# Norm applies ahead of the w1 scale, low halves of w1 and w2 on GpSimd, loads ahead of the transposing transfers, and a last tile in two banks

## The chip, the cores and the metric

The kernel runs on one core of a Trainium2 chip. A core has a matrix engine (TensorE, PE in the profile; its weight loads are listed as PEld), a vector engine (VectorE, DVE), an activation engine (ScalarE, ACT), a general engine (GpSimd, POOL) and a sequencer that here issues the transfers (SyncE, SP). The engines run their own queues in order and meet through semaphores. The metric is the device time of one execution in microseconds, the median of the timed runs.

## The reference

The input x has S = 2048 rows of D = 448 numbers. The output is the sum of x, a spectral branch and a mixer branch, both fed by a layer norm over the row.

```python
def _A_ref(x, w_r, w_i):                       # spectral branch
    X = jnp.fft.rfft2(x, axes=(-2, -1))
    return jnp.fft.irfft2(X * (w_r + 1j * w_i), s=(S, D), axes=(-2, -1))

def _B_ref(x, w1, w2, w3, w4):                 # mixer branch
    h = _gelu(_layernorm(x) @ w1)
    # four column groups of h, shifted by +1, -1, +2 and -2 rows, zeros at the ends
    hs = jnp.concatenate([g0, g1, g2, g3], axis=-1) @ w2
    x1 = x + hs
    return x1 + _gelu(_layernorm(x1) @ w3) @ w4

return x + _A_ref(_layernorm(x), A_w_r, A_w_i) + _B_ref(_layernorm(x), B_w1, ...)
```

w1 and w2 are 448 x 448, w3 is 448 x 1792, w4 is 1792 x 448. All inputs are float32.

## The kernel before

**Tiles.** Row 16·a + b of x lies in partition a of tile b, so there are 16 tiles of 128 rows, and a shift by one row is a step to the neighbouring tile. The tiles are worked in four groups, `GRP = [[14, 15, 0, 1], [2, 3, 4, 5], [6, 7, 8, 9], [10, 11, 12, 13]]`. Two tiles share one load (`xt`, 448 KB).

**Number format.** Products run in float16 with each operand split into a high half (the value rounded to float16) and a low half (what is left). A product is three matmuls: high by high, high by low, low by high. A weight is first multiplied by a power of two, which comes from its sum of squares: `squares` (L233 to L237) sums on ACT, `powers` (L239 to L252) reduces on DVE, sums over the partitions with a matmul by ones and makes the powers of two by integer steps on DVE. `split_w` (L257 to L260) then writes the high half on ACT (L258) and the low half on DVE (L259), for w1, w2, w3 and w4 alike.

**Stages.** At the start, PE runs 28 warm-up matmuls on zeros (L732) while the first loads land, and two more behind the product of w1's scale. For each group, `norm1` (L291) takes the row statistics on DVE, makes a rough inverse root with a few tiny DVE steps that end in `nma` (L305), and applies them to the four tiles of the group (L310 on ACT, L312 on DVE or POOL, as its list of engines says). A refinement of the inverse root, tiny steps on POOL (L321 to L341), corrects the scale later. `transpose_split` (L356) turns the four tiles by PE transposes into banks of the accumulation memory (L362), writes the high half on ACT (L365) and the low half on DVE (L366). `w1_in` (L395) makes the products with w1 (matmuls L398), `w1_unit` (L408) applies gelu (L416), splits the result into `hs` (L417, L418) and sends it through a transposing transfer into `hT` (L421). `w2_tile` (L425) makes the product with w2 for one row tile, with four shifted sources (L437), and adds it to x (L439). `ln2` (L442) is the second norm, whose split rows go through transposing transfers too (L473). `front` and `back` (L674, L688) are the w3 and w4 products of a group of two row tiles G, in seven steps of two column blocks f; the w4 products of a row tile accumulate in one bank over all 14 blocks (L696), which is read at the last step (L703), and the result is stored (L705). The spectral branch runs in between: a fold and a first transform (L491 to L528), 16 chunks (L575 to L629) and the inverse (L641 to L669). PE has the w3 and w4 products of the groups as filling for these stages.

**What sets the order.** The program is written in a Python order, and a scheduler of the framework orders the instructions of each engine by priorities, dependences and its own planned time. `behind(key)` makes what is issued inside it come after a named instruction in that plan; `prio` sets a priority. Banks come from tags with two buffers each (tr, mm, acc, sp). SP issues all loads, stores and transposing transfers, one after another in its own order. Eight semaphores count their completions, and each transfer waits for the one eight before it.

**The order around the start.** SP loads group 0 of x, w1 (`w1s`, four parts, the last in two halves), group 1, w2, group 2 and the first two row blocks of w3 (`w3raw`). Group 3 of x and the third row block of w3 are issued behind the last transposing transfer of group 0 (L783 to L785), the last row block of w3 and half of w4 behind those of group 1 (L801 to L804). The scale of w1 (L757) is written behind the norm of group 0 (L756). Group 0's w1 products use three of the four row blocks of w1 first (L768); the last follows between transposes of group 1 (L776 to L780). The low halves of w2 are made when the statistics of group 2 are through (L794 to L796).

Of the kernel before, what the change touches and what calls it, by code (L numbers as in the profile page):

```python
# [20 lines left out]
NB, NC = 16, 16  # L21
# [4 lines left out]
SHIFT = [1, -1, 2, -2]  # L26
WARM = 28, 2
ZPRE = 2.0 ** -7
# [91 lines left out]
def body(tc, nc, x, wf, w1, w2, w3, w4, c_g, c_n, c_small, out):  # L120
# [41 lines left out]
    def xb(b):  # L162
        return xt[b // 2][:, b % 2]
# [69 lines left out]
    def squares(col, src, junk=None):  # L233

        n = src.shape[-1]
        junk = x2mem if junk is None else junk
        A.activation(out=junk[:src.shape[0], :n], in_=src, func=AF.Square, scale=2.0 ** -20, accum_out=col)  # L237

    def powers(m, n, key, tag="acc"):  # L239

        t = pc.tile([128, 2], F32, name=f"pt{key}")
        V.tensor_reduce(out=t[:, 0:1], in_=m[:, :n], axis=AX.X, op=ALU.add)
        pm = bank(tag, f"pm{key}")
        i = T.matmul(pm[:, 0:1], ones, t[:, 0:1], start=True, stop=True)
# [46 lines left out]
    def norm1(g, apply):  # L291
# [15 lines left out]
        for k, b in enumerate(bs):  # L307
            y_, m_ = y[:, n + k:n + k + 1], nm[:, k:k + 1]
            if apply[k] is A:
                A.activation(out=xb(b), in_=xb(b), func=AF.Identity, scale=y_, bias=m_)  # L310
            else:
                i = apply[k].tensor_scalar(out=xb(b), in0=xb(b), scalar1=y_, scalar2=m_, op0=ALU.mult, op1=ALU.add)  # L312
                if apply[k] is V:
                    after["n", g] = (i.ins,)
# [41 lines left out]
    def transpose_split(srcs, dst, key, ts=range(4), at=0, tags=("tr",) * 4):  # L356
        c = slice(128 * at, 128 * at + 128 * len(srcs))
        for t in ts:
            pt = bank(tags[t], f"pt{key}{t}")
            w = 128 if t < 3 else 64  # L360
            for i, s in enumerate(srcs):
                T.transpose(pt[:w, 128 * i:128 * i + 128], s[:, 128 * t:128 * t + w], ident)  # L362
            pt = pt[:w, :128 * len(srcs)]
# [30 lines left out]

    def w1_in(g, i, pm, ts):  # L395
        for t in ts:
            for wi, xi in ((0, 0), (0, 4), (4, 0)) if t < 3 else ((0, 0), (4, 0)):
                T.matmul(pm[:, :D], xTs[g][:, xi + t, 128 * i:128 * i + 128], w1p[:, wi + t],  # L398
                         start=t == 0 and wi + xi == 0, stop=t == 3 and wi == 4)

# [3 lines left out]

    hs_buf.append(x2mem[:, F:F + 1024].rearrange("p (i k n) -> p i k n", i=2, k=4))
    P.memset(hs_buf[HS].rearrange("p i k n -> p (i k) n")[:, :, 112:], 0.0)

    def w1_unit(g, i, pm=None):  # L408
        if pm is None:
            pm = bank(("mm", "mm", "acc", "acc")[i], f"pw1_{g}{i}")  # L410
            w1_in(g, i, pm, range(4))
        c = CS[GRP[g][i]]
        pm = pm[:, :D]
        pv_ = pm.rearrange("p (k n) -> p k n", k=4)
        h = hs_buf[c % (HS if g == 3 else HS + 1)]
        A.activation(out=pm, in_=pm, func=AF.Gelu_apprx_tanh, scale=gsc[:, c:c + 1])  # L416
# [271 lines left out]
    def back(G, fp):  # L688
        h = hs.pop((G, fp))
        if fp == 0:  # L690
            acc[G] = [bank("acc", f"acc{G}{i}") for i in range(2)]
        for i in range(2):
            for f in (2 * fp, 2 * fp + 1):
                for n, (hi, wi) in enumerate(((0, 0), (0, 1), (1, 0))):
                    o = 256 * (f % 2) + 128 * i
                    m = T.matmul(acc[G][i][:, :D], h[:, hi, o:o + 128], w4p[0][:, wi, f],  # L696
                                 start=f == 0 and n == 0, stop=f == 13 and n == 2)
                    after["m", G, fp] = (m.ins,)
            b = 2 * G + i
            if fp == 6 and b in rest:  # L700
                t = rest.pop(b)
                with prio(EVAC):
                    V.scalar_tensor_tensor(out=t, in0=acc[G][i][:, :D], scalar=p34[:, 1:2], in1=t,  # L703
                                           op0=ALU.mult, op1=ALU.add)
                    SY.dma_start(ov[:, b], t)  # L705
            elif fp == 6:
# [26 lines left out]

    warm_up(WARM[0])
    m1, m2, m3, m4 = (pc.tile([128, n], F32, name=f"m{i}") for i, n in ((1, 4), (2, 1), (3, 4), (4, 7)))
    junk4 = row().bitcast(F16)[:, :2 * D]
    V.memset(m2, 0.0)
# [15 lines left out]

    for t in range(4):
        squares(m1[:, t:t + 1], w1s[:, t])
    n1 = [norm1(0, [P, V, A, V])]  # L756
# [188 lines left out]
```

## Time and profile before

| | |
|---|---|
| timed runs | 424.54, 425.66, 427.21 us; median 425.66 |
| profiled execution | 428.35 us, of which the span from the first to the last instruction is 426.6 |
| TensorE clock granted, mean | 0.996 |
| PE matmuls | busy 412.9 us, 97% of the span, 3289 instructions |
| DVE | busy 291.7 us, 68% |
| ACT | busy 248.6 us, 58% |
| POOL | busy 107.8 us, 25% |
| transfers | 47.6 MB, mean 112 GB/s |

The profile is one execution. A line such as `L312 POOL TENSOR_SCALAR xt<-xt,vy,nma x8: 704/715/2584` reads: line 312 of the kernel, on GpSimd, a tensor by scalar operation from xt, vy and nma into xt, eight times, shortest, median and longest in ns. In the timeline a row begins with its start and its length in us; a group of equal instructions in a row is one row with their number behind an x. In square brackets stands how long the engine had been idle before, and which instruction ended the wait. SPq, POOLq and the like are the sequencers' own rows. The row of a transfer is the time that SP spent on issuing it; when its bytes had landed is told apart from it.

### The profile page before, as it was taken

How to read it: one execution, taken by the hardware profiler on the slowest of the kernel's cores; microseconds unless marked ns; L12 is line 12 of the kernel's file. 1: busy time of each engine (PE TensorE's matmuls, PEld its weight loads, DVE VectorE, ACT ScalarE, POOL GpSimd, SP SyncE). 2: the span in 40 equal slices, each digit the busy share in tenths (PEclk: the TensorE clock that was granted, in tenths of full speed). 3: DMA queues.
4: the chain of work that ended last, by engine and by line, in shares of the span. 5: the costliest groups of instructions: out<-in, count | busy, mean ns of one | idle time of the engine just before them, and what ended most of it. 6: DMA issues, size and time to landing. Idle time of an engine off the chain costs nothing.

```text
span 426.6 us, 8457 instructions
## 1 busy us (share of the span) xinstructions
PE 412.9 (97%) x3289; PEld 288.1 (68%) x3289; DVE 291.7 (68%) x619; ACT 248.6 (58%) x428; POOL 107.8 (25%) x191
## 2 busy tenths in 40 slices
PE   7989899999999999999999999999999999999996
PEld 3545465666657777777778878787776767577764
DVE  3889399989854567663478889876899619852122
ACT  4588479974486767553288888864444424522331
POOL 2446520101122964420021211220454303200000
PEclk9999899999999999999999999999999999999999
DMA  8939995454682247223145665520001103430001
GB/s 278 314 75 210 189 274 155 80 126 86 88 198 64 88 137 255 90 83 104 33 112 158 154 166 153 137 70 15 2 2 48 40 2 111 149 129 28 18 0 45
DMA packets 51688, 47.61 MB, mean 112 GB/s; under 512 B 33920, under 2 KB 46912, under 8 KB 51648
## 3 DMA queue, kind: packets, MB, share of 16 engines
q1 hardware_dynamic: 51648, 47.07, 41.6%
q8 instruction: 26, 0.43, 0.4%
q14 instruction: 14, 0.11, 0.1%
HBM read 35.52 MB, written 3.67 MB: 92 GB/s over the span
## 4 chain that ended last, share of the span: by engine, by line
PE 54%; DVE 8%; issue 3%; DMA 3%; ACT 1%; POOL 1%; DVEq 0%; SPq 0%
PE pw L372 22%; PE acc L696 22%; PE ps L523 3%; PE pu L625 2%; PE pp L580 2%; PE px L597 2%; DMA xr<-x 2%; DVE xt L669 1%; DMA out<-xr 1%; DVE xr L480 1%; DVE vh L661 1%; DVE e L657 1%; DVE x2mem L480 1%; DVE e L655 1%; DVE U L638 1%
## 5 line engine op out<-in xcount | busy, mean ns | idle before, releaser
L372 PE MATMUL pw<-x2mem,w3p 128*128 128x256 f16 x1232 | 152.6, 273 | 0.0
L696 PE MATMUL acc<-w4p,hf 128*128 128x448 f16 x672 | 140.1, 353 | 1.0 <-DVE hf L684 1.0
L372 PEld LDWEIGHTS <-w3p 128*128 128x128 f16 x1232 | 118.9, 98 | 24.6 <-issue 0.9
L696 PEld LDWEIGHTS <-hf 128*128 128x128 f16 x672 | 65.2, 98 | 51.9 <-DVE hf L684 1.9
L684 DVE SCALAR_TENSOR_TENSOR hf<-pw,h,hf 128x512 f16<-128x512 f32 x56 | 41.9, 747 | 60.8 <-ACT hf L683 60.5
L681 ACT ACTIVATE pw<-pw,pe 128x512 f32<-128x512 f32 x56 | 36.6, 654 | 68.2 <-PE pw L372 67.2
L437 PE MATMUL pw<-w2p,h 112*128 112x448 f16 x192 | 41.0, 357 | 2.3 <-DMA h<-hs 2.2
L683 ACT ACTIVATE hf<-pw,h 128x512 f16<-128x512 f32 x56 | 38.4, 686 | 1.5
L398 PE MATMUL pw<-w1p,xT 128*128 128x448 f16 x176 | 36.4, 360 | 1.4 <-ACT xT L365 0.8
L606 POOL TENSOR_TENSOR z<-te 128x450 f32<-128x450 f32 x16 | 16.3, 1017 | 73.9 <-DVE te L604 73.9
L437 PEld LDWEIGHTS <-h 112*128 112x128 f16 x192 | 18.9, 99 | 18.2 <-DMA h<-hs 3.2
L398 PEld LDWEIGHTS <-xT 128*128 128x128 f16 x176 | 17.3, 100 | 18.4 <-issue 2.0
L653 POOL TENSOR_TENSOR e<-e 128x226 f32<-128x226 f32 x16 | 13.5, 842 | 56.5 <-ACT e L650 45.3
L587 ACT ACTIVATE pf<-pp 64x450 f16<-64x450 f32 x32 | 17.3, 540 | 16.6 <-DVE pf L588 8.1
L588 DVE TENSOR_TENSOR pf<-pp,pf 64x450 f16<-64x450 f32 x32 | 19.9, 621 | 5.3 <-ACT pf L587 5.0
L650 ACT ACTIVATE e<-pe 128x452 f32<-128x452 f32 x16 | 8.7, 547 | 15.6 <-DVE vh L661 12.3
L602 ACT ACTIVATE te<-px 64x450 f32<-64x450 f32 x32 | 17.2, 538 | 0.5
L660 ACT ACTIVATE vh<-e 128x448 f16<-128x448 f32 x16 | 9.2, 574 | 14.2 <-DVE e L658 10.7
L503 POOL TENSOR_TENSOR xr<-xf 128x452 f32<-128x452 f32 x8 | 9.2, 1155 | 30.9 <-issue 23.4
L514 DVE TENSOR_TENSOR xh<-f,xh 128x452 f16<-128x452 f32 x16 | 11.8, 780 | 6.8 <-ACT xh L513 6.8
L506 POOL TENSOR_TENSOR f<-xr 128x452 f32<-128x452 f32 x16 | 15.9, 1017 | 0.6
L416 ACT ACTIVATE pw<-pw,gsc 128x448 f32<-128x448 f32 x16 | 9.3, 606 | 10.7 <-POOL xt L312 5.7
(155 smaller groups left out, 600.3 us busy)
## 6 DMA issues: line engine op xcount, KB each, us to landing
wc<-wf SPq DMA_DIRECT2D x32, 225.0 KB, 3.5
wl<-wf SPq DMA_DIRECT2D x8, 450.0 KB, 3.8
xt<-x SPq DMA_DIRECT2D x8, 448.0 KB, 5.2
xf<-x SPq DMA_DIRECT2D x8, 448.0 KB, 3.8
w3raw<-w SPq DMA_DIRECT2D x3, 896.0 KB, 11.3
xr<-x SPq DMA_DIRECT2D x12, 224.0 KB, 2.6
out<-xr SPq DMA_DIRECT2D x12, 224.0 KB, 1.9
gn<-c_g SPq DMA_DIRECT2D x16, 128.0 KB, 3.3
```

The costliest lines, as they stand in the source:

```text
L372: T.matmul(ps_out, wp[:, wi + t, cols], xT[:, xi + t, tok], start=t == 0 and wi + xi == 0, stop=t == 3 and wi == 4)
L398: T.matmul(pm[:, :D], xTs[g][:, xi + t, 128 * i:128 * i + 128], w1p[:, wi + t], start=t == 0 and wi + xi == 0, stop=t == 3 and wi == 4)
L437: T.matmul(pm[:, :D], hT[g][:112, 4 * hi + k, o:o + 128], w2p[:, wi, k], start=n == 0, stop=n == 11)
L506: P.tensor_tensor(out=f[:, :, k:k + 2].rearrange("p b s d -> p s b d"), in0=u[:, :, 0], in1=u[:, :, 1], op=op)
L587: A.activation(out=hi, in_=src, func=AF.Copy)
L588: V.tensor_tensor(out=lo, in0=src, in1=hi, op=ALU.subtract)
L602: A.activation(out=e[64 * h:64 * h + 64], in_=px_[64 - 64 * h:128 - 64 * h, :2 * DF], func=AF.Copy)
L606: P.tensor_tensor(out=z, in0=t[:, 0], in1=t[:, 1], op=ALU.add)
L681: A.activation(out=pm, in_=pm, func=AF.Gelu_apprx_tanh, scale=r3)
L683: i = A.activation(out=h[:, 0], in_=pm, func=AF.Copy, scale=h3)
L684: j = V.scalar_tensor_tensor(out=h[:, 1], in0=pm, scalar=h3, in1=h[:, 0], op0=ALU.mult, op1=ALU.subtract)
L696: m = T.matmul(acc[G][i][:, :D], h[:, hi, o:o + 128], w4p[0][:, wi, f], start=f == 0 and n == 0, stop=f == 13 and n == 2)
```

## The change

Five things are changed.

The order of loads: group 3 of x and the third row block of w3 go out right behind the first two row blocks of w3, and the second half of w1's last row block goes out behind group 1 of x.

The start: w1's scale (`powers`) is placed behind the norm of group 0, the two warm-up matmuls behind the scale are left out, the squares write their unused result to another buffer (`xr`), the four transposes of one bank are chained behind those of the bank before, group 0's w1 products run over all four row blocks in passes (high by high, low x, low w) over the four units, and group 1's transposes follow them as three blocks and one. The gelus of group 0 are placed behind group 1's split.

The low halves: w1's row blocks 2 and 3 and all four of w2 are split with a new path, in which GpSimd multiplies the weight in place by its scale, ACT copies it to the high half, and GpSimd subtracts.

Buffers and banks: two `hs` buffers lie in `x2mem` instead of one, the units of group 1 and the transposes of group 2 use other bank tags, w2's scale uses 64 free columns of a bank of group 0, and `w2_tile` takes the shifts in the order 2, 0, 1, 3.

The end: the last row tile (b = 15) accumulates its two halves of 224 columns in two banks, and reads and stores each half by itself.

```diff
-WARM = 28, 2
+WARM = 28
...
-    for h in range(2):
-        SY.dma_start(w1s[64 * h:64 * h + 64, 3], w1[384:448])
+    SY.dma_start(w1s[0:64, 3], w1[384:448])
     load_x(1)
+    SY.dma_start(w1s[64:128, 3], w1[384:448])
...
     load_w3([0, 1])
+    load_x(3)
+    load_w3([2])
...
-        junk = x2mem if junk is None else junk
+        junk = xr.bitcast(F16) if junk is None else junk
...
-        pm = bank(tag, f"pm{key}")
+        pm = bank(tag, f"pm{key}") if isinstance(tag, str) else tag
...
-    def split_w(hi, lo, src, s):
+    def split_w(hi, lo, src, s, low=None):
+        if low is P:
+            P.tensor_scalar(out=src, in0=src, scalar1=s, scalar2=0.0, op0=ALU.mult, op1=ALU.add)
+            i = A.activation(out=hi, in_=src, func=AF.Copy)
+            j = P.tensor_tensor(out=lo, in0=src, in1=hi, op=ALU.subtract)
+            return i.ins, j.ins
...
-            for i, s in enumerate(srcs):
-                T.transpose(pt[:w, 128 * i:128 * i + 128], s[:, 128 * t:128 * t + w], ident)
+            with behind("T", key) if ("T", key) in after else contextlib.nullcontext():
+                for i, s in enumerate(srcs):
+                    m = T.transpose(pt[:w, 128 * i:128 * i + 128], s[:, 128 * t:128 * t + w], ident)
+            after["T", key] = (m.ins,)
...
+    def w1_in(g, units, ts, passes=range(3)):
+        for p in passes:
+            for t in ts:
+                for i, pm in units:
+                    wi, xi = ((0, 0), (0, 4), (4, 0))[p]
+                    if t < 3 or p != 1:
+                        T.matmul(pm[:, :D], xTs[g][:, xi + t, 128 * i:128 * i + 128], w1p[:, wi + t],
+                                 start=t == 0 and p == 0, stop=t == 3 and p == 2)
...
-    hs_buf.append(x2mem[:, F:F + 1024].rearrange("p (i k n) -> p i k n", i=2, k=4))
-    P.memset(hs_buf[HS].rearrange("p i k n -> p (i k) n")[:, :, 112:], 0.0)
+    for o in (0, 1024):
+        hs_buf.append(x2mem[:, o:o + 1024].rearrange("p (i k n) -> p i k n", i=2, k=4))
+        P.memset(hs_buf[-1].rearrange("p i k n -> p (i k) n")[:, :, 112:], 0.0)
...
-            pm = bank(("mm", "mm", "acc", "acc")[i], f"pw1_{g}{i}")
+            pm = bank(("tr" if g == 1 else "mm", "acc")[i // 2], f"pw1_{g}{i}")
...
-        for k in range(4):
+        for k in (2, 0, 1, 3):
...
+            if G == 7:
+                acc[G].append(bank("sp", "acc72"))
...
+            c = D // 2 if b == NB - 1 else D
+            parts = [(slice(o, o + c), acc[G][i + o // c][:, 0:c]) for o in range(0, D, c)]
+            for r, to in parts:
+                with behind("m", G, fp) if (G, fp) == (7, 6) and ("m", G, fp) in after else contextlib.nullcontext():
+                    for f in (2 * fp, 2 * fp + 1):
+                        for n, (hi, wi) in enumerate(((0, 0), (0, 1), (1, 0))):
+                            o = 256 * (f % 2) + 128 * i
+                            m = T.matmul(to, h[:, hi, o:o + 128], w4p[0][:, wi, f, r],
+                                         start=f == 0 and n == 0, stop=f == 13 and n == 2)
...
+                    for r, to in parts:
+                        V.scalar_tensor_tensor(out=t[:, r], in0=to, scalar=p34[:, 1:2], in1=t[:, r],
+                                               op0=ALU.mult, op1=ALU.add)
+                        SY.dma_start(ov[:, b, r], t[:, r])
...
-                        tags=("tr", "tr", "acc", "acc"))
+                        tags=("mm", "mm", "tr", "tr") if g == 2 else ("tr", "tr", "acc", "acc"))
...
     n1 = [norm1(0, [P, V, A, V])]
-    s1, r1 = powers(m1, 4, "1")
-    with behind("p1"):
-        warm_up(WARM[1])
+    with behind("n", 0):
+        s1, r1 = powers(m1, 4, "1", "mm")
...
-    T1(0)
     for t in range(4):
+        with behind("p1"):
+            T1(0, [t])
         with behind("a0", t):
-            after["w1", t] = split_w(w1p[:, t], w1p[:, 4 + t], w1s[:, t], s1)
+            after["w1", t] = split_w(w1p[:, t], w1p[:, 4 + t], w1s[:, t], s1, P if t > 1 else V)
...
-    for t in range(3):
-        for k in range(4):
-            w1_in(0, k, first[k], [t])
+    for t in range(4):
+        w1_in(0, list(enumerate(first)), [t])
     n1[0][0]()
+    with behind("w1", 1):
+        n1.append(norm1(1, [P, V, A, V]))
     with behind("w1", 3):
-        n1.append(norm1(1, [P, V, A, V]))
         squares(m2[:112], flat(w2s[:112]))
-        s2, r2 = powers(m2, 1, "2")
+    T1(1, range(3))
+    with behind("n", 1):
+        s2, r2 = powers(m2, 1, "2", first[0][:, 448:512])
     with behind("p2"):
-        T1(1, range(2))
-        for k in range(4):
-            w1_in(0, k, first[k], [3])
-        T1(1, range(2, 4))
-    for k in range(4):
-        w1_unit(0, k, first[k])
-    with behind("h", 0, 3):
-        load_x(3)
-        load_w3([2])
-    n1[1][0]()
+        T1(1, [3])
...
+    n1[1][0]()
     with behind("a1"):
+        w1_unit(0, 0, first[0])
         n1.append(norm1(2, [P, V, A, P]))
-    with behind("a1"), behind("c", 2):
+    with behind("a1"), behind("n", 2):
+        for k in range(1, 4):
+            w1_unit(0, k, first[k])
+    with behind("na", 2):
         for k in range(4):
-            split_w(w2p[:, 0, k], w2p[:, 1, k], w2s[:112, k], s2[:112])
+            split_w(w2p[:, 0, k], w2p[:, 1, k], w2s[:112, k], s2[:112], P)
```

More of the change, by code (lines that the diff above doesn't have):

```diff
@@ L309, in norm1 @@
             if apply[k] is A:
-                A.activation(out=xb(b), in_=xb(b), func=AF.Identity, scale=y_, bias=m_)
+                i = A.activation(out=xb(b), in_=xb(b), func=AF.Identity, scale=y_, bias=m_)
+                after["na", g] = (i.ins,)
             else:
@@ L393, in h_at @@
         return 128 * i if g else 144 * i + 16
[L395 to L399, printed above, removed]
+    def w1_in(g, units, ts, passes=range(3)):
[6 more added lines that the diff above has]
+                                 start=t == 0 and p == 0, stop=t == 3 and p == 2)
     hs_buf = [p1.tile([128, 2, 4, 128], F16, name=f"hs{i}") for i in range(HS)]
@@ L403, in body @@
         P.memset(t.rearrange("p i k n -> p (i k) n")[:, :, 112:], 0.0)
-    hs_buf.append(x2mem[:, F:F + 1024].rearrange("p (i k n) -> p i k n", i=2, k=4))
-    P.memset(hs_buf[HS].rearrange("p i k n -> p (i k) n")[:, :, 112:], 0.0)
+    for o in (0, 1024):
+        hs_buf.append(x2mem[:, o:o + 1024].rearrange("p (i k n) -> p i k n", i=2, k=4))
+        P.memset(hs_buf[-1].rearrange("p i k n -> p (i k) n")[:, :, 112:], 0.0)
     def w1_unit(g, i, pm=None):
         if pm is None:
-            pm = bank(("mm", "mm", "acc", "acc")[i], f"pw1_{g}{i}")
-            w1_in(g, i, pm, range(4))
+            pm = bank(("tr" if g == 1 else "mm", "acc")[i // 2], f"pw1_{g}{i}")
+            w1_in(g, [(i, pm)], range(4))
         c = CS[GRP[g][i]]
@@ L414, in w1_unit @@
         pv_ = pm.rearrange("p (k n) -> p k n", k=4)
-        h = hs_buf[c % (HS if g == 3 else HS + 1)]
+        h = hs_buf[c % (HS if g == 3 else HS + 2)]
         A.activation(out=pm, in_=pm, func=AF.Gelu_apprx_tanh, scale=gsc[:, c:c + 1])
@@ L691, in back @@
             acc[G] = [bank("acc", f"acc{G}{i}") for i in range(2)]
+            if G == 7:
+                acc[G].append(bank("sp", "acc72"))
         for i in range(2):
[L693 to L698, printed above, removed]
-            b = 2 * G + i
+            b = 2 * G + i
+            c = D // 2 if b == NB - 1 else D
[7 more added lines that the diff above has]
+                                         start=f == 0 and n == 0, stop=f == 13 and n == 2)
+                after["m", G, fp] = (m.ins,)
             if fp == 6 and b in rest:
@@ L702, in back @@
                 with prio(EVAC):
-                    V.scalar_tensor_tensor(out=t, in0=acc[G][i][:, :D], scalar=p34[:, 1:2], in1=t,
-                                           op0=ALU.mult, op1=ALU.add)
-                    SY.dma_start(ov[:, b], t)
+                    for r, to in parts:
+                        V.scalar_tensor_tensor(out=t[:, r], in0=to, scalar=p34[:, 1:2], in1=t[:, r],
+                                               op0=ALU.mult, op1=ALU.add)
+                        SY.dma_start(ov[:, b, r], t[:, r])
             elif fp == 6:
@@ L732, in warm_up @@
             T.matmul(wps, wsrc[:, 0:128], wsrc, start=True, stop=True)
-    warm_up(WARM[0])
+    warm_up(WARM)
     m1, m2, m3, m4 = (pc.tile([128, n], F32, name=f"m{i}") for i, n in ((1, 4), (2, 1), (3, 4), (4, 7)))
     junk4 = row().bitcast(F16)[:, :2 * D]
+    V.memset(m1, 0.0)
     V.memset(m2, 0.0)
@@ L752, in w4_split @@
         split_w(w4p[0][:, 0, f:f + 2], w4p[0][:, 1, f:f + 2], w4raw[:, f:f + 2], s4)
-    for t in range(4):
+    for t in range(3):
         squares(m1[:, t:t + 1], w1s[:, t])
+    squares(m1[:64, 3:4], w1s[:64, 3])
     n1 = [norm1(0, [P, V, A, V])]
-    s1, r1 = powers(m1, 4, "1")
-    with behind("p1"):
-        warm_up(WARM[1])
+    with behind("n", 0):
+        s1, r1 = powers(m1, 4, "1", "mm")
     h_alloc(0)
     first = [bank("mm" if k < 2 else "sp", f"pw1_0{k}") for k in range(4)]
-    T1(0)
     for t in range(4):
+        with behind("p1"):
+            T1(0, [t])
         with behind("a0", t):
-            after["w1", t] = split_w(w1p[:, t], w1p[:, 4 + t], w1s[:, t], s1)
+            after["w1", t] = split_w(w1p[:, t], w1p[:, 4 + t], w1s[:, t], s1, P if t > 1 else V)
     h1 = pc.tile([128, 1], F32, name="h1")
     V.tensor_scalar(out=h1, in0=s1, scalar1=2.0 ** -5, scalar2=None, op0=ALU.mult)
-    for t in range(3):
-        for k in range(4):
-            w1_in(0, k, first[k], [t])
+    for t in range(4):
+        w1_in(0, list(enumerate(first)), [t])
     n1[0][0]()
+    with behind("w1", 1):
+        n1.append(norm1(1, [P, V, A, V]))
     with behind("w1", 3):
-        n1.append(norm1(1, [P, V, A, V]))
         squares(m2[:112], flat(w2s[:112]))
-        s2, r2 = powers(m2, 1, "2")
+    T1(1, range(3))
+    with behind("n", 1):
+        s2, r2 = powers(m2, 1, "2", first[0][:, 448:512])
     with behind("p2"):
-        T1(1, range(2))
-        for k in range(4):
-            w1_in(0, k, first[k], [3])
-        T1(1, range(2, 4))
-    for k in range(4):
-        w1_unit(0, k, first[k])
-    with behind("h", 0, 3):
-        load_x(3)
-        load_w3([2])
-    n1[1][0]()
+        T1(1, [3])
     s12 = pc.tile([128, 4], F32, name="s12")
```

## The prediction

> **What bounds the kernel now.** I read the busy shares first. TensorE (PE) works 97% of the span, and the chain that ended last runs mostly through its two big matmul loops, so time can be won only where PE stands idle or where its work changes.
>
> ```profile
> PE 412.9 (97%) x3289; PEld 288.1 (68%) x3289; DVE 291.7 (68%) x619; ACT 248.6 (58%) x428; POOL 107.8 (25%) x191
> PE 54%; DVE 8%; issue 3%; DMA 3%; ACT 1%; POOL 1%; DVEq 0%; SPq 0%
> ```
>
> The table of windows tells where it is idle (columns: window, its length, busy us and instructions of PE, PEld, DVE, ACT, POOL, then TensorE clock, DMA share, GB/s).
>
> ```profile
> 20.00:30.00 10.00, 8.18 (x49) 4.37 (x47) 7.98 (x29) 8.66 (x17) 5.04 (x20) 1.00 0.43 89
> 30.00:40.00 10.00, 9.84 (x59) 5.71 (x58) 9.22 (x24) 7.06 (x14) 6.35 (x16) 1.00 0.73 192
> 40.00:50.00 10.00, 7.82 (x33) 3.48 (x32) 5.87 (x19) 4.29 (x6) 3.71 (x11) 0.83 1.22 172
> ...
> 70.00:80.00 10.00, 10.00 (x56) 5.29 (x55) 10.00 (x18) 10.00 (x18) 0.00 (x0) 1.00 0.02 3
> ...
> 150.00:200.00 50.00, 50.00 (x451) 37.91 (x450) 30.16 (x44) 29.56 (x53) 18.35 (x20) 1.00 0.40 129
> ```
>
> From 50 us to about 400 PE hardly stops, so a microsecond won before 50 should arrive at the end whole, unless DVE and ACT, both full in 70 to 80, take it back. Nearly all of the change lies before 50. I then looked for the waits there in the timeline (start, length, engine, line, idle before and its releaser).
>
> ```profile
> 9.98 0.16 DVE L242 TENSOR_REDUCE pt<-m 128x1 f32<-128x4 f32 x1 [1.24 <-ACT x2mem L237]
> ...
> 11.31 1.97 PE L362 MATMUL pta<-ident,xt 128*128 128x128 f32 x16 [0.29 <-POOL xt L312]
> ...
> 23.03 1.97 PE L362 MATMUL pta<-ident,xt 128*128 128x128 f32 x16 [0.65 <-POOL xt L312]
> ...
> 25.79 0.58 PE L398 MATMUL pw<-w1p,xT 128*128 128x448 f16 x2 [0.79 <-ACT xT L365]
> ...
> 33.23 1.06 SPq L192 DMA_DIRECT2D xt<-x  x2
> 33.70 3.28 POOL L312 TENSOR_SCALAR xt<-xt,vy,nma 128x448 f32<-128x448 f32 x2
> ```
>
> ```profile
> 44.38 2.51 PE L437 MATMUL pw<-w2p,h 112*128 112x448 f16 x9 [2.19 <-DMA h<-hs]
> ```
>
> A matmul's length on the page includes its pipeline; its price on PE is the distance from start to start, 0.189 us for 448 columns. By that measure PE lost 0.45 before the transposes at 11.31, 0.53 before the first w1 matmul at 13.65, 2.63 in 20 to 30, 0.50 in 30 to 40, and 4.05 in 40 to 50. The last is a 2.35 us wait for h (group 1's transposing transfers) and then nine matmuls at 0.373 instead of 0.189, 1.67 us, where the clock column shows 0.83.
>
> **The change, step by step.**
>
> *Applies first.* Today the reduction L242 waits for the fourth square of w1 (done about 9.95) and stands on DVE ahead of the last step of the norm, L305, and so of the applies L312. L303 is through at 8.74; with the reduction behind the applies, L305 starts near 8.75. POOL, which has two 0.2 us steps of its refinement first, applies at about 9.5, ends near 10.5, and the transposes start at 10.57: 0.74 earlier. The scale's product stays at 10.2 (it still waits for the same squares), but the steps behind it on DVE, which today wait from 10.6 to 11.43 for the applies to end, run at once, and so does ACT's first hi half: first w1 matmul at 12.48, against 13.65. **−1.17**, the two removed warm-up matmuls (0.43) and the 0.45 and 0.53 included.
>
> *w1 stage in one piece.* The 44 w1 matmuls of group 0, pass by pass over four banks, need 44 × 0.189 = 8.3 us, 12.48 to 20.8, with the group-1 transposes behind them. The waits of 20 to 30 (0.81 for the POOL apply, 0.96 and 0.41 for xT, 0.29 for h) go: 2.63. What is late next is POOL's apply of group 1, ready at 20.6 by its queue against 20.8: cover of only 0.2. I leave 0.15. **−2.5**.
>
> *Loads ahead of transposes.* In 33 to 44 two x loads and a w3 row block (0.45, 0.45, 0.90 MB) travel beside group 1's transposes. Those then took up to 7.8 us to land, group 0's, alone, 3.1 to 3.4; one issue held SP for 5.3 us instead of 1.25. Moved behind the first w3 loads, the three go out at 10 to 12.4 and, 1.8 MB at the 340 GB/s of 10 to 20, land about 5.3 us after today's last (21.8), at 26 to 27. Each transfer waits for the one eight before it, so SP gets to group 0's transposes in time. The h0 transposes are issued from 27.9: cover about 1 us. Group 1's, issued 33.9 to 37.7 with nothing beside them, land 1.4 us before PE needs them. So the 2.35 and the 1.67 behind it go, and 0.3 for a POOL apply. I leave 1.0 for three new small waits in 32 to 35 (0.49 h0, 0.21, 0.30 the w2 low halves). 4.55 − 1.0 = **−3.5**.
>
> *Low halves on GpSimd.* Six L259 (0.68 each, −4.1 us) leave DVE for six pairs on POOL. The multiply has a near row, L312 at 0.715 median. The subtraction of f16 from f32 has none: from below the same 0.7, from above the 2.584 of the one apply that stretched; I take L606, two inputs of nearly the same size:
>
> ```profile
> L606 POOL TENSOR_TENSOR z<-te x16: 978/982/1297, 217.5 to 286.6; 128x450 f32<-128x450 f32 x16
> ```
>
> Six pairs are 6 × (0.715 + 0.98) = 10.2 us. POOL is busy 5.00, 5.04 and 6.35 in the three windows from 10 to 40; the 6.35 holds 1.87 of stretch. 14.5 + 10.2 = 24.7 of 30: it just fits, since w1's low halves are ready at 17.4 and 18.5 for passes that need them at 18.5 and 20.0, and w2's come out about as PE wants them. The cost is the 0.3 above. But behind each subtraction stand the applies and scales of the next groups, so once the queue is full (above some 1.4 us each) each extra 0.1 costs about 6 × 0.1 less the odd gap, some 0.5 us.
>
> The 2.584 apply ran while DVE did L259 from 32.98 to 34.85. The Trainium skill, "SBUF — State Buffer", Who interferes with whom, says that VectorE with two SBUF inputs and a GpSimd read shut each other out for a whole instruction. The trace agrees, with 2.584 against 0.715. By that rule adding GpSimd work next to a full DVE is a risk; yet the L259 of w2, which have two SBUF inputs, are the ones removed, and L366 and L418, with one input in PSUM, are what remains, so the sum by it is the same.
>
> *Tail.* The last row tile's 42 matmuls of 448 columns become 84 of 224. Nearest row: L597 at 225 columns starts every 0.097 us, so a pair costs 0.194 for 0.189: +0.21 over 42. The first half's eviction and store now run beside the second half's last six matmuls; the last eviction shrinks from 0.684 to about 0.45 (bounds 0.34 and 0.68), the last store from 224 KB (issue to landing 1.94) to 112 KB. Sum −0.1, from −0.4 to +0.3.
>
> ```profile
> 422.31 1.44 DVE L703 SCALAR_TENSOR_TENSOR x2mem<-acc,p,x2mem 128x448 f32<-128x448 f32 x2 [1.62 <-PE acc L696]
> ```
>
> *The rest*, two more h buffers, w2's order of shifts, other banks, h2's transposes between those of the second norm, I cost at nothing: PE is full from 50 on. PE reaches 60 to 130 seven us sooner and finds DVE and ACT full there with h transposes only 0.4 us ahead, so I give back 0.8.
>
> Sum: −1.17 − 2.5 − 3.5 − 0.1 + 0.8 = **−6.5**. The profiled execution took 428.35 (span 426.6 and 1.75 around it), 2.7 over the timed median of 425.66; profiled I expect 421.9, timed **419.2**.
>
> **Rivals.**
>
> *A. The half clock was the profile's own.* If timed runs don't hold the 1.67, the gain is 4.8: 420.9. The Trainium skill, "TensorE: Matmul & The Clock Gate", Part 1, has the rate halved after an idle window of about 3.4 us that runs free of the kernel. The trace shows half rate after 2.35 idle, so by it the loss would hang on where the window falls.
>
> *B. GpSimd becomes the wait.* At 1.7 to 2.2 us per subtraction PE waits for w2's low halves: gain 4 down to 0.5, 421.7 to 425. For it: POOL at 82% on paper; against: what stretched it goes.
>
> *C. Transposes still meet loads.* Group 0's, if the moved loads end 2 us later than I think, or group 2's behind w4's loads: one 2 to 3 us wait and its half clock, gain 2 to 3.3, 422.4 to 423.7.
>
> *D. Taken back in 60 to 100,* where DVE is busy 9.94 and 10.00 per 10: gain 0 to 1, 425.
>
> *E. Slower.* Same mechanism as B at its far end: subtractions at 3.2 us each, above the stretched apply but below the 3.758 that the slowest L653 took. Past 2.3 us the gain is gone; at 3.2 it is 0.9 × 4.8 = 4.3 worse, 430. Against: only two rows of the page are stretched so.
>
> That the change doesn't do what it says I set aside: the built order shows the loads, applies and halves moved.
>
> **Chances.** Forecast 0.54, A 0.14; B 0.10, C and D 0.10 together; E and anything like it 0.12. A measurement tells 1%, 4.3 us, from nothing. So faster 0.68, same 0.20, slower 0.12. Range 416.0 (1 us of the give-back and the small waits do not come, and the tail at its best) to 425.5 (all of B to D); E lies outside.
>
> **What would show it.** First L362 at 10.6, first L398 at 12.5 and unbroken to 20.8; w3raw's third block landed by 27; no h transposes over 4 us before 40; clock 1.00 in 40 to 50; POOL's new subtractions near 1 us. If L437 first waits for POOL's w2 half, B; for h, C; if the early gain is there at 60 but gone at 130, D.

## The result and the profile after

The changed kernel takes **420.06 us** (median of 5 runs, 419.97 to 420.40) against 425.66; the ratio is 0.9864 (95% interval 0.9838 to 0.989), 5.6 us or 1.4% faster. Forecast were 419.2 and a range of 416.0 to 425.5. The profiled execution took 420.40, its span is 418.6.

The page of the changed kernel begins with the busy shares; TensorE works 98% of a span that is 8 us shorter than the profiled one before.

```profile
span 418.6 us, 8535 instructions
...
PE 409.8 (98%) x3329; PEld 291.7 (70%) x3329; DVE 291.6 (70%) x615; ACT 248.1 (59%) x428; POOL 118.6 (28%) x204
```

The same windows as before, of the changed kernel (window, length, busy us and instructions of PE, PEld, DVE, ACT, POOL, then TensorE clock, DMA share, GB/s):

```profile
10.00:20.00 10.00, 10.00 (x60) 6.09 (x60) 8.67 (x27) 6.65 (x11) 8.65 (x23) 1.00 1.04 352
20.00:30.00 10.00, 10.00 (x60) 5.66 (x59) 7.97 (x27) 8.54 (x17) 7.14 (x25) 1.00 0.53 200
30.00:40.00 10.00, 9.23 (x55) 5.28 (x54) 8.80 (x16) 9.89 (x18) 8.21 (x22) 1.00 0.97 177
40.00:50.00 10.00, 10.00 (x56) 5.44 (x55) 8.02 (x31) 7.08 (x10) 6.45 (x20) 1.00 1.10 228
50.00:60.00 10.00, 10.00 (x62) 5.98 (x61) 9.94 (x30) 5.97 (x12) 1.83 (x7) 1.00 0.86 207
```

PE is full in 10 to 30 and again in 40 to 50, at clock 1.00. The row 30 to 40 holds what is left, and GpSimd is now busy 24.0 of the 30 us from 10 to 40; the forecast had 24.7. The timeline of the start and of the w2 stage (start, length, engine, line; in brackets the idle time before and its releaser):

```profile
10.35 1.97 PE L370 MATMUL pta<-ident,xt 128*128 128x128 f32 x16
...
12.24 8.48 PE L410 MATMUL pw<-w1p,xT 128*128 128x448 f16 x44
...
16.15 2.03 POOL L262 TENSOR_TENSOR w1p<-w1s,w1p 128x448 f16<-128x448 f32 x2
...
20.57 1.47 PE L370 MATMUL pta<-ident,xt 128*128 128x128 f32 x12
```

```profile
32.42 3.01 POOL L262 TENSOR_TENSOR w2p<-w2s,w2p 112x448 f16<-112x448 f32 x3
...
33.69 0.36 PE L450 MATMUL pw<-w2p,h 112*128 112x448 f16 x1 [0.77 <-DMA h<-hs]
```

The transposes start at 10.35 (forecast 10.57), the first w1 matmul at 12.24 (12.48), all 44 run in one piece, group 1's transposes follow without a gap. What is left before 50 is one wait for h, 0.9 us, at 33.69. The end of the kernel:

```profile
414.27 1.60 DVE L723 SCALAR_TENSOR_TENSOR x2mem<-acc,p,x2mem 128x448 f32<-128x448 f32 x3 [1.25 <-PE acc L716]
414.98 1.32 SPq L725 DMA_DIRECT2D out<-x2mem  x3
```

The third row block of w3 lands at 26.75 (forecast: by 27), and the transposing transfers issued before 40 take 3.1 to 3.7 us but for the last, which takes 4.78. So the steps came out as described. But the profiled executions differ by 8.0 us and the timed medians by 5.6. Where the other 2.4 went is the first question for the experiments; the second is what each part is worth.

### The profile page after: what moved, and what is told of

The parts are those of the page before. It is cut to its first block, busy times and chain, and to the rows that moved or that the text cites. A ratio compares the mean times of both kernels' runs of the same rounds, so it can differ in the third digit from the quotient of the medians.

```text
span 418.6 us, 8535 instructions
## 1 busy us (share of the span) xinstructions
PE 409.8 (98%) x3329; PEld 291.7 (70%) x3329; DVE 291.6 (70%) x615; ACT 248.1 (59%) x428; POOL 118.6 (28%) x204
## 4 chain that ended last, share of the span: by engine, by line
PE 72%; DVE 14%; DMA 6%; issue 5%; POOL 1%; ACT 1%; SPq 1%; POOLq 0%; DVEq 0%
PE pw L381 25%; PE acc L716 22%; PE pw L450 7%; PE pw L410 6%; PE ps L536 3%; PE pu L638 2%; PE pp L593 2%; PE px L610 2%; DMA xr<-x 1%; DVE w4p L265 1%; DMA out<-xr 1%; PE pta L370 1%; DMA x2mem<-y 1%; DVE xt L682 1%; DVE sta L289 1%
## 5 line engine op out<-in xcount | busy, mean ns | idle before, releaser
L716 PE MATMUL acc<-w4p,hf 128*128 128x448 f16 (+1 forms) x714 | 140.0, 341 | 0.7 <-DVE hf L697 0.7
L716 PEld LDWEIGHTS <-hf 128*128 128x128 f16 x714 | 69.2, 98 | 49.2 <-DVE hf L697 1.6
L450 PE MATMUL pw<-w2p,h 112*128 112x448 f16 x192 | 40.1, 352 | 0.8 <-DMA h<-hs 0.8
L410 PE MATMUL pw<-w1p,xT 128*128 128x448 f16 x176 | 35.3, 352 | 0.0
L681 PE MATMUL py<-vh,csm 128*128 128x448 f16 x48 | 13.5, 352 | 1.5 <-DVE vh L674 0.7
```

The lines of the kernel that those rows point to most:

```text
L450: T.matmul(pm[:, :D], hT[g][:112, 4 * hi + k, o:o + 128], w2p[:, wi, k], start=n == 0, stop=n == 11)
L716: m = T.matmul(to, h[:, hi, o:o + 128], w4p[0][:, wi, f, r], start=f == 0 and n == 0, stop=f == 13 and n == 2)
```

## The experiments

Each kernel below was timed against the kernel before on the same chip, so the ratio to that is the measure; differences are given in us of 425.6. A kernel with one thing undone is planned anew by the framework, so its orders can change elsewhere too; where that matters it is said.

**The kernel before once more.** No edit.

> The kernel before, unchanged, to see what its own executions differ by. Theory: the 2.35 us wait for h and the half clock behind it (1.67) are not in every execution. The profile on record (428.35, clock 0.996) had both; the timed ones between 424.5 and 427.2 should show a clock of 0.999 or 1.000 where they are near 425 and 0.996 where they are above 427, and a new profile should show a smaller loss in 40 to 50 us. Rival: the half clock is in all of them (clock 0.996 each time) and the spread of 3 us comes from elsewhere.

Measured: 425.70 (425.14 to 427.81, 12 runs), ratio 1.0012 (0.9998 to 1.0027). In these 12 runs and the 24 of the same kernel beside them the clock was 0.998 to 1.000, never 0.996, also in those of 427 and 428. The new profile (425.79, span 424.0) shows, in the windows and the timeline:

```profile
40.00:50.00 10.00, 9.49 (x51) 4.71 (x49) 6.15 (x20) 7.65 (x11) 4.79 (x14) 1.00 1.09 186
70.00:80.00 10.00, 9.78 (x65) 6.13 (x63) 9.96 (x22) 8.70 (x17) 0.46 (x2) 1.00 0.15 27
90.00:100.00 10.00, 9.82 (x64) 6.05 (x63) 10.00 (x19) 7.09 (x10) 0.22 (x1) 1.00 0.23 44
```

```profile
42.07 1.88 PE L437 MATMUL pw<-w2p,h 112*128 112x448 f16 x9 [0.51 <-DMA h<-hs]
```

```profile
80.66 1.69 PE L437 MATMUL pw<-w2p,h 112*128 112x448 f16 x8 [0.88 <-DMA h<-hs]
```

Here the wait for h is 0.51 and no half clock follows. The execution on record had the unlucky size: its third row block of w3 took 8.96 us from issue to landing (34.34 to 43.30), this one 7.33 (33.69 to 41.02), and in both the first transposing transfer landed 1.0 later. In exchange a PE that comes sooner waits again at 80.66 and in 90 to 100, which the one on record did not. So the theory holds in that the half clock and most of the wait belong to the execution on record. It fails in that the runs above 427 have no lower clock: the spread of the runs, 3 us at clock 1.000, comes from elsewhere, and its cause is open. The wait for h is seen in two profiles only.

TensorE's lost time, by start to start, in three profiles. The new profile of the kernel before is called the usual one from here on, since its 425.79 lies at the median of its runs:

| stage | before, on record | before, usual | after |
|---|---|---|---|
| first w1 matmul starts | 13.65 | 13.01 | 12.24 |
| lost in 20 to 30 | 2.63 | 2.63 | 0.41 |
| lost in 30 to 50 | 4.55 | 1.18 | 1.29 |
| lost in 50 to 200 | 1.68 | 2.97 | 1.10 |
| lost in 200 to the end | 3.11 | 3.26 | 2.91 |
| span | 426.6 | 424.0 | 418.6 |

Against the usual execution the span falls by 5.4, close to the timed 5.6.

**The loads behind group 0's transposing transfers again.**

```diff
     load_w3([0, 1])
-    load_x(3)
-    load_w3([2])
...
+    with behind("h", 0, 3):
+        load_x(3)
+        load_w3([2])
     with behind("na", 2):
```

> The changed kernel with one thing undone: group 3 of x and the third row block of w3 go out behind group 0's transposing transfers again. Theory: group 1's transposes, issued around 36 to 40, travel beside these loads, land 6 to 8 us after their issue instead of 3.4 to 4.8, and TensorE waits for h about 2 us, with a half clock behind it in some executions: 422 to 423.7 against 420.1. Rival: w2's products have other work before them by now and the load order is worth under 1 us: 420 to 421.

Measured: 425.88 (425.20 to 427.80), ratio 1.0013 (0.9999 to 1.0027). The whole gain is gone, about 6 us, up to three times what was expected, and not at the expected place. Timeline and windows of this kernel:

```profile
53.09 1.70 ACT L236 ACTIVATE xr<-w3raw 128x1792 f16<-128x1792 f32 x1 [5.60 <-DMA w3raw<-w]
...
54.91 0.16 DVE L241 TENSOR_REDUCE pt<-m 128x1 f32<-128x4 f32 x1 [4.97 <-ACT xr L236]
...
55.12 0.38 PE L243 MATMUL pm<-pt,ones 128*128 128x1 f32 x2 [1.99 <-DVE pt L241]
```

```profile
40.00:50.00 10.00, 10.00 (x58) 5.63 (x57) 6.49 (x20) 6.33 (x10) 6.41 (x22) 1.00 1.15 211
50.00:60.00 10.00, 7.45 (x35) 3.57 (x34) 4.76 (x16) 6.37 (x11) 0.87 (x2) 0.82 1.08 290
60.00:70.00 10.00, 10.00 (x46) 4.83 (x45) 9.94 (x32) 8.81 (x10) 0.90 (x2) 0.84 0.58 168
```

PE doesn't wait for h at all in 40 to 50, though the transfers of group 1 are as late as before (up to 8.7 us from issue to landing). It waits at 55 for the scale of w3: its last row block, queued on SP behind those transfers, lands at 53.0 instead of 47.9, ACT sums its squares at 53.1 instead of 48.5, and the product with ones (L243) stands in PE's queue ahead of transposes that then run at once. ACT, idle for 5.60 us, and VectorE, idle for 4.97, are held in the same way: the splits of transposes that are long done, on which the next w1 matmuls wait, come behind that row block's instructions in their queues. So the theory's mechanism falls, and the rival's size with it: in the changed kernel the load order is needed for w3's scale.

How the wait becomes 6 us is shown only in part. In this profile PE loses 3.3 us by waits in 50 to 70 and 2.8 by a half clock from 56.34 on. But the runs at clock 0.999 and 1.000 are hardly faster (425.20 to 425.64). What all of them could share is VectorE: behind its 4.97 idle us it is busy 9.94 and 10.00 of 10 us in 60 to 70 and 70 to 80, so it can't catch up there. No run takes that apart.

**The load order alone, in the kernel before.**

```diff
     load_w3([0, 1])
+    load_x(3)
+    load_w3([2])
...
-    with behind("h", 0, 3):
-        load_x(3)
-        load_w3([2])
```

> The kernel before with the load order alone: group 3 of x and the third row block of w3 right behind the first two row blocks of w3. Theory, terms that add up: the wait for h around 44 and the half clock go, 1.9 to 3.5 us: 422.2 to 423.8. Rival: group 0's transposes now meet the loads, or the next wait (GpSimd's apply behind VectorE's w2 halves) takes the place: within 1 us of before, 425.

Measured: 423.61 (423.24 to 424.01), ratio 0.9964 (0.995 to 0.9979), 1.5 us. The losses in 40 to 50 and in 70 to 100 go (0.70 and 1.47 to 0.02 and 0.11). Some of it is paid at group 0's transfers, as the expectation's rival says: PE loses 0.85 at the first w2 matmul instead of 0.32.

```profile
29.46 0.36 PE L439 MATMUL pw<-w2p,h 112*128 112x448 f16 x1 [0.68 <-DMA h<-hs]
```

That w1 starts at 13.36, 0.35 later than in the usual execution, is not the edit's: w1's last load lands at 8.88, before the first of the moved loads is issued (9.09), and the execution on record has 9.17 for that landing and 13.65 for the start, the usual one 8.44 and 13.01. A part that is worth 1.5 alone is worth 6 with the others: without it they gain nothing, since PE comes sooner only to wait for w3's scale.

**The low halves on VectorE again**, all six, and then w1's two alone.

```diff
-            after["w1", t] = split_w(w1p[:, t], w1p[:, 4 + t], w1s[:, t], s1, P if t > 1 else V)
+            after["w1", t] = split_w(w1p[:, t], w1p[:, 4 + t], w1s[:, t], s1)
...
-            split_w(w2p[:, 0, k], w2p[:, 1, k], w2s[:112, k], s2[:112], P)
+            split_w(w2p[:, 0, k], w2p[:, 1, k], w2s[:112, k], s2[:112])
```

> The changed kernel with the low halves of w1 (row blocks 2 and 3) and of w2 on VectorE again. Theory: they are off the path; VectorE has 4.1 us more before 35, and the applies and evictions behind them come later by a part of that: 420 to 421.5. Rival one: VectorE, full from 50 to 70, passes all of it on: 424. Rival two: the GpSimd chain costs more than it saves, and the time falls to 419.

> The changed kernel with w1's two low halves on VectorE and w2's four still on GpSimd; TensorE's order is the same. With all six on VectorE the norm of group 1 came 1.2 us later and TensorE waited 0.96 at 20.4 us. Theory: that is the whole worth of the low halves on GpSimd, and w2's share is nothing: 421.0, like all six (421.1). Rival: w2's four matter as well, since VectorE does them at 32.7 to 35.2 just ahead of group 1's splits: 420.4 to 420.7 here.

Measured: all six 421.14, ratio 0.9903 (0.9885 to 0.9921); w1's two alone 421.93, ratio 0.99 (0.9883 to 0.9916), where the changed kernel beside it has 0.9874. Both cost about 1.1 us against the changed kernel (1.0 to 1.7 by ratios or medians). The ratios' intervals overlap a little; the six runs with w1's two (421.54 to 422.48) all lie above the five of the changed kernel on that chip (420.65 to 421.03). Timeline with w1's two on VectorE:

```profile
18.36 0.65 DVE L265 SCALAR_TENSOR_TENSOR w1p<-w1s,pe,w1p 128x448 f16<-128x448 f32 x1
...
19.89 0.16 DVE L311 SCALAR_TENSOR_TENSOR nma<-mva,vy 128x4 f32<-128x4 f32 x1
...
20.27 1.17 POOL L319 TENSOR_SCALAR xt<-xt,vy,nma 128x448 f32<-128x448 f32 x1
...
21.50 0.77 PE L370 MATMUL pta<-ident,xt 128*128 128x128 f32 x5 [0.80 <-POOL xt L319]
```

The two low halves delay the norm of group 1 on VectorE (nma at 19.89, in the changed kernel 18.72), the applies and group 1's transposes with it. w2's four make no difference that can be told (0.9903 with them, 0.99 without), and VectorE does not pass its 4.1 us on.

**Each subtraction on GpSimd twice.**

```diff
+            P.tensor_tensor(out=lo, in0=src, in1=hi, op=ALU.subtract)
             j = P.tensor_tensor(out=lo, in0=src, in1=hi, op=ALU.subtract)
```

> The changed kernel with each of the six subtractions on GpSimd done twice, so that a low half costs about 2.0 us there instead of 1.0; the result is the same. Theory, by the price in the prediction (0.5 us for each 0.1 past 1.4): 6 tenths times 0.5, about 3 us: 423, up to 425. Rival, now that the low halves on VectorE cost only 1.1 us: GpSimd has slack or the order gives way, and it costs under 1.5: 420.3 to 421.5.

Measured: 424.09 (423.72 to 426.23), ratio 0.9971 (0.9955 to 0.9988): 4.6 us by the ratio, 4.0 by the medians. The theory's place is right and its price is somewhat low. Of PE's 4.5 us of new losses 2.5 lie in 10 to 40 and 2.2 in 70 to 80, where VectorE, in the new plan's order, reaches the sum of a w2 tile late:

```profile
76.99 1.29 PE L451 MATMUL pw<-w2p,h 112*128 112x448 f16 x6 [1.27 <-DVE xt L453]
```

So the changed kernel stands near the edge: one more microsecond for each of six instructions takes most of the gain. How the late sum at 77 follows from GpSimd isn't shown.

**The scale ahead of the norm again.** Only VectorE's order changes, by one instruction.

```diff
-    with behind("n", 0):
-        s1, r1 = powers(m1, 4, "1", "mm")
+    s1, r1 = powers(m1, 4, "1", "mm")
```

> The changed kernel with the reduction of w1's scale ahead of the norm of group 0 on VectorE again; the order on all other engines is the same. Theory: the applies start at 10.0 instead of 8.9 and the transposes and the first w1 matmul come 0.7 to 1.0 later, all of which reaches the end: 420.8 to 421.1. Rival: a wait further on (group 0's transposing transfers at 32.7, 0.9 us) swallows it: within 0.3 of 420.1.

Measured: 420.77 (420.69 to 421.07), ratio 0.9886 (0.9867 to 0.9906). The first w1 matmul starts at 12.81 instead of 12.24, and the span grows by 0.7. The intervals of the two ratios overlap, so the times alone don't tell it. The profile follows the theory: seven profiles with the new start, of this and other kernels here, have the first w1 matmul at 12.14 to 12.34, and in this one PE stands 0.72 us ahead of the transposes (10.91), until GpSimd's apply ends at 10.85.

**The w1 stage as before**, in the changed kernel: three row blocks, half of group 1's transposes, the fourth row block, the other half.

```diff
-    for t in range(4):
+    for t in range(3):
         w1_in(0, list(enumerate(first)), [t])
     n1[0][0]()
-    with behind("w1", 1):
+    with behind("w1", 3):
         n1.append(norm1(1, [P, V, A, V]))
...
-    T1(1, range(3))
...
     with behind("p2"):
-        T1(1, [3])
+        T1(1, range(2))
+        w1_in(0, list(enumerate(first)), [3])
+        T1(1, range(2, 4))
```

> The changed kernel with group 0's w1 stage as before: three row blocks, then two blocks of group 1's transposes, the fourth row block, the rest of the transposes, and no gelu held back. Loads, applies, low halves and tail stay as changed. Theory: the 2.5 us of waits in 20 to 30 come back and reach the end: 422 to 422.6. Rival one: they come back but the stage from 50 to 100 had a reserve by VectorE and ScalarE: under 1 us, 420.5 to 421. Rival two: like with the loads undone, the wait that shows is another one and larger: over 423.5.

Measured: 428.11 (425.61 to 430.60, 12 runs), ratio 1.0052 (1.0028 to 1.0077): slower than the kernel before. It isn't a clean undoing: the passes stay, and the gelus are no longer held back. The plan now puts two of group 1's statistics on VectorE ahead of group 0's applies, where they wait for a load:

```profile
9.51 1.15 DVE L289 BATCH_NORM_STATS2 sta<-xt 128x6 f32<-128x448 f32 x2 [0.43 <-DMA xt<-x]
...
11.62 0.38 PE L245 MATMUL pm<-pt,ones 128*128 128x1 f32 x2 [1.79 <-DVE pt L243]
```

PE loses 2.68 in 20 to 30, about the 2.63 of before, though at other places: it no longer waits ahead of the transposes, but three times for xT between w1 matmuls (27.66, 28.48 and 29.79). That bears out the kind of the term and only roughly its size. PE loses 3.1 more by 20, and 1.4 more in 30 to 50. The half clock shows in 10 to 20 and in 30 to 40:

```profile
10.00:20.00 10.00, 8.38 (x43) 5.28 (x44) 8.63 (x30) 6.56 (x12) 8.89 (x28) 0.83 1.05 337
20.00:30.00 10.00, 7.97 (x50) 4.71 (x48) 4.98 (x14) 6.31 (x12) 5.45 (x17) 1.00 0.60 222
30.00:40.00 10.00, 9.85 (x48) 5.18 (x47) 6.55 (x19) 6.22 (x12) 3.13 (x7) 0.83 0.85 153
```

Part of the time is that half clock: the four runs at 0.999 and 1.000 take 425.6 to 426.2, as long as the kernel before, and the other eight are longer. So without it, too, this kernel loses the whole gain, through the later start and the waits together.

**The last tile in one bank again.**

```diff
-            if G == 7:
-                acc[G].append(bank("sp", "acc72"))
...
-            c = D // 2 if b == NB - 1 else D
+            c = D
```

> The changed kernel with the last row tile in one bank again (42 matmuls of 448 columns, one eviction, one store). Theory: the two halves are worth 0.1 us, from 0.4 better to 0.3 worse: 419.8 to 420.5. Rival: eviction and store of half the size end the span earlier by most of a microsecond: 420.8 to 421.

Measured: 420.67 (420.21 to 420.98), ratio 0.9882 (0.9862 to 0.9902). This isn't told apart from the changed kernel. The profiles show both sides of the sum: from the first chunk matmul to the end of the last matmul PE takes 214.99 with two banks (200.39 to 415.38) and 214.69 with one (200.22 to 414.91), 0.3 more; from there to the end of the span it is 3.2 with two and 3.5 with one. The timeline with one bank:

```profile
413.81 0.68 DVE L721 SCALAR_TENSOR_TENSOR x2mem<-acc,p,x2mem 128x448 f32<-128x448 f32 x1 [1.24 <-PE acc L714]
414.52 1.47 SPq L723 DMA_DIRECT2D out<-x2mem  x2
414.95 0.69 DVE L721 SCALAR_TENSOR_TENSOR x2mem<-acc,p,x2mem 128x448 f32<-128x448 f32 x1 [0.45 <-PE acc L714]
```

Two evictions of 0.68 here; with two banks the three together take 1.60, so the two halves cost 0.46 each, as forecast.

**An attempt at a better version**: the scale's reduction between VectorE's two applies (`hook` calls `powers` for w1), ACT's first high half ahead of its first eviction; and the same with the last tile cut at 336 columns.

```diff
+            if hook and k == 3:
+                with behind("n", g):
+                    hook()
...
+            with behind("h1") if (key, t) == ("a0", 0) else contextlib.nullcontext():
+                i = A.activation(out=dst[:w, t, c], in_=pt, func=AF.Copy)
...
-            c = D // 2 if b == NB - 1 else D
+            cuts = (0, 336, D) if b == NB - 1 else (0, D)
```

> The changed kernel itself, on the chip of the three that follow, as their measure: 420.1 again, within 0.3.

> An attempt at a better version: the changed kernel with the reduction of w1's scale between VectorE's two applies of group 0 instead of behind them, and with ScalarE's first high half of w1 ahead of its first eviction of transposes; TensorE's, GpSimd's and the transfers' orders are the same. The scale's product then starts at about 9.5 instead of 9.99 and the first w1 matmul at 11.8 instead of 12.24. Theory: 0.2 to 0.4 of it reach the end, since GpSimd's apply of group 1 has 0.3 us of slack ahead of the transposes at 20.57: 419.7 to 419.9. Rival: the slack is the bound, no difference: 420.1.

> The same, and the last row tile cut into 336 and 112 columns instead of 224 and 224, so that the last eviction and the last store have half the size. Theory: 0.1 to 0.2 less than the run with the first high half ahead: 419.5 to 419.8. Rival: 112-column matmuls are held by their weight loads (0.098 each), 42 x 0.05 = 2 us more: 421.5 to 422.

Measured, on one chip, where the kernel before takes 426.58: the changed kernel 420.96 (ratio 0.9874, 0.9856 to 0.9892), the first attempt 420.97 (0.987, 0.9849 to 0.989), both together 420.68 (0.9871, 0.9853 to 0.9889). Nothing is gained that can be told. The changed kernel takes 0.9 more here than in the result, and so does the kernel before (426.58 against 425.66). In the profiles the first w1 matmul starts at 12.34, 12.68 and 12.11; the last two have the same start edit, so they differ by more from one execution to the next (0.57) than the 0.44 that it was to bring. The 112-column matmuls cost nothing visible. No version here beats the changed kernel.

## Why the prediction came out as it did

**Applies first, −1.17.** The transposes came 0.74 earlier in the forecast; undoing that step alone costs 0.57 at the first w1 matmul and 0.7 of the span in the profile, and can't be told by the times. From the usual execution to the changed one the first w1 matmul moves by 0.77, from the one on record by 1.41. Right in kind; the start on record was 0.64 later than usual, with w1's last load landing 0.73 later.

**The w1 stage in one piece, −2.5.** Lost time in 20 to 30 falls from 2.63 to 0.41. Right. What the step did not say is that it needs the low halves of w1 off VectorE: with those two there, group 1's transposes wait 0.96, and 1.1 us of the time comes back. The prediction gave the relief of VectorE no value and the GpSimd path a cost of 0.3; the runs say a gain of 1.1.

**The loads, −3.5.** This is the term that failed in size, and the reason lies in its first row: the 2.35 of waiting and the 1.67 of half clock were taken from the one profiled execution as the cost of every execution. In the usual execution the wait is 0.51 (0.67 lost) and there is no half clock; the time in 30 to 50 is 1.18 lost before and 1.29 after. The order of loads alone is worth 1.5, most of it by waits at 80 and 90 that the profile on record does not show. Rival A had this cause, at a chance of 0.14, but kept the 2.35: 420.9. The measured time lies midway between it and the forecast. Inside the changed kernel the load order has a second worth that no step named: w3's last row block and the scale product that stands ahead of ready matmuls on PE.

**The low halves.** The subtraction took 1.03 us, near the 0.98 of the row that was taken and far from the upper end of 2.584. The price past the edge was put at 0.5 us for 0.1; at twice 1.03, 0.66 past it, it was 4.0 to 4.6 instead of 3.3. On the Trainium skill, "SBUF — State Buffer", Who interferes with whom: by the rule the longest apply on GpSimd should fall once VectorE's low halves of w2 are gone, and it falls from 2.584 to 1.173. That isn't a test of the rule: with all six low halves on VectorE again the longest is 1.172, since there none of them runs beside an apply. A closer sign is that in the changed kernel two small GpSimd steps of 0.20 us (L336, L344) take 0.67 and 0.66 at 12.34 and 13.55, beside VectorE's low halves of w1's first two row blocks, which have two SBUF inputs. No subtraction was stretched (1.028 to 1.037).

**The tail, −0.1.** Not told apart from nothing.

**Given back, +0.8.** This did not happen: DVE is busy 9.94 and 9.97 of 10 us in 50 to 60 and 60 to 70, ACT 10.00 and 9.70 in 60 to 70 and 70 to 80, yet PE loses 1.10 in 50 to 200, less than the 2.97 of the usual execution before. Rivals C and D did not occur in the changed kernel, and C occurs in the load order alone (0.5 us).

The forecast of 6.5 thus holds one term, the loads, that was about 2 too large, against a give-back of 0.8 that did not come; with the smaller differences of the other terms that leaves it 0.9 above the measured 5.6. That it came so near is in part luck. The terms were read from an execution of 428.35 and their sum taken off a median of 425.66; against the profiled execution the gain is 8.0, more than the 6.5, and against the median 5.6, less.

## What to carry to other kernels

Before a stall in one profiled execution becomes a term of a sum, look whether that execution is usual: this one was 0.6% above the median, and its mean clock of 0.996 was below that of all 36 later runs. A part's worth depends on the others: the load order gives 1.5 us alone and 6 us with the rest, since without it a PE that comes sooner only meets the next late thing. And look for instructions that wait in the queue ahead of work that is ready, such as a one-column product for a scale; their inputs set the time though they cost next to nothing themselves.

## What the runs showed of the hardware

Transposing transfers that are issued behind plain loads landed after these. In eight places of five profiles the first one landed 0.8 to 2.5 us after the last load issued ahead of it: 41.02 and 42.02, 56.54 and 57.38 in the usual execution before, 43.30 and 44.33, 58.75 and 59.58 in the one on record, 42.34 and 44.86, 57.67 and 58.57 with the loads back, 52.64 and 53.45 in the changed kernel, 54.61 and 55.48 with the subtractions twice. Whether they wait for the loads or only share the way with them isn't told by this. With no load in flight ahead of them they take 3.0 to 3.8 us from issue to landing, behind loads up to 10.2. SP's issue row then stretches too, from 1.25 up to 5.7 us, and everything behind it on SP waits.

The half clock comes in spells of one length, and whether one comes changes from one execution to the next. The windows below show the spell of the execution on record, then the two of the old w1 stage, then the one with the loads back, which is twice as long.

```profile
45.48:48.89 3.41, 3.41 (x11) 1.36 (x9) 1.78 (x10) 0.00 (x0) 1.68 (x4) 0.50 1.28 132
```

```profile
12.92:16.33 3.41, 3.41 (x15) 2.10 (x13) 3.41 (x15) 3.20 (x7) 3.33 (x10) 0.50 1.06 340
...
29.99:33.40 3.41, 3.41 (x11) 1.41 (x10) 3.41 (x10) 0.50 (x1) 0.00 (x0) 0.50 0.57 107
```

```profile
56.34:63.17 6.83, 6.34 (x17) 2.50 (x18) 6.77 (x31) 5.11 (x9) 1.68 (x4) 0.50 1.06 226
```

Three of them begin 1.1 to 1.3 us after PE had stood idle for 2.19, 1.79 and 1.99 us; the one at 29.99 follows three shorter waits (1.17, 0.27 and 0.58). A single wait of up to 1.28 us had none behind it in the profiles here. Where PE sets the time a spell of 3.41 costs half its length, an estimate of 1.7 us, and 0.004 of the mean clock. The 12 runs with the old w1 stage lie on such steps, though the spells themselves are seen in the profiled one alone: 425.6 to 426.2 at 0.999 and 1.000, 426.9 and 427.5 at 0.996 and 0.995, 428.7 to 429.3 at 0.992 and 0.991 (the profiled one, with its two spells, is of these), 430.6 at 0.988. The Trainium skill, "TensorE: Matmul & The Clock Gate", Part 1, ties the half clock to an idle window of about 3.4 us that runs free of the kernel. The length of the spells agrees with that window and the change between executions fits a window that runs free, but the idle times that were enough here are shorter than it. With the loads back the clock varied from 0.991 to 1.000 as well, but the times hardly did (425.9 at 0.992, 425.6 at 1.000); there VectorE, busy 9.94 in 60 to 70, may be the limit behind it.
